# A sparse-attention and expert kernel: start-up work redistributed, fewer weight transfers, and a new planner order

## The chip, the cores and the metric

The kernel runs on one core of a Trainium2 chip. Such a core has TensorE (PE, matmuls; its weight loads stand apart as PEld), VectorE (DVE), ScalarE (ACT), GpSimd (POOL) and SyncE (SP, which here only issues DMAs and loads registers), and sixteen DMA engines. The metric is the device time of one execution in microseconds; lower is better.

## The reference, cut to what matters

Two attention layers follow each other, for B = 4 batches of S = 768 tokens in float32. The first has H = 8 heads of D = 64; tokens form 24 blocks of 32, and a block of queries sees its neighbours, the first and the last block, and three sampled blocks. The first and the last block of queries see everything.

```python
mask = np.abs(blk_i - blk_j) <= 1
mask |= (blk_i == 0) | (blk_j == 0) | (blk_i == 23) | (blk_j == 23)
for qb in range(24):
    for kb in sampled_blocks[qb]:          # 3 each
        mask[qb*32:(qb+1)*32, kb*32:(kb+1)*32] = True
x = softmax(where(mask, q @ k.T / 8, -1e9)) @ v      # heads side by side: (B, 768, 512)
# second layer: 4 experts, the best 2 per token by x @ w_gate
for e in range(4):
    a = softmax(causal((x @ wq[e]) @ (x @ wk[e]).T / 8))
    out += weight_of(e) * (a @ (x @ wv[e]) @ wo[e])
```

## The kernel before

**Steps and planner.** The kernel does not run its steps in the order of its source. Each step is handed to `Plan.add` with its engine (or a choice of engines), an estimated duration, what it reads and writes, and a priority, mostly the place of its unit in a list of units. `Plan.run` then walks through a modelled time: whenever an engine is free it takes the ready step with the lowest priority number, and the instructions are issued on each engine in just that order. On the chip every engine runs its own list strictly in order; semaphores hold an instruction back until its inputs are there. Limits in the plan: `window` (how many units ahead of the oldest unfinished one a step may be), `look` (the same for transfers), `near` (how far TensorE may reach past the first ready step for one with the same array shape, since a change of shape is costed at `SWITCH`). `AHEAD` lets score matmuls run with a priority of four units earlier.

**Stage 1, sparse attention.** For each batch, `load_keys` puts all keys into the tile `KK` (L471), `load_values` the values into `VN` with a column of ones (copies at L427 and L431; for later batches L513) and stores them to a scratch tensor `scr` in DRAM (L523). `ends` handles the first and the last block of queries for two pairs of heads (unit G): scores L671, maximum L678, exponentials L681, transposes L689, weighted sum L699, normalising L709 to L713, transpose L718. `tiles` handles 128 queries (four blocks) and four heads (unit U; two units a tile, six tiles a batch): scores L749 (first four tiles of batch 0, straight from `KK`) or L756, maximum L763, exponentials L768, transposes L774, weighted sum L788, normalising L798 to L800, transpose L805, split into two halves L443 and L444.

**What a tile needs first.** `gather_keys` copies its sampled blocks of keys to a key buffer, by block numbers read into registers (`load_registers`, L323, from the row `si`). There are three key buffers and a tile takes two. In batch 0 each block is a step of its own that POOL (L568), DVE (L568) or ACT (L566) may take. `gather_values` fills `va` and `vb`, two of each: in batch 0 POOL copies the neighbour blocks and the first and last block out of `VN` (L599, 32 to 96 partitions at a time); the sampled blocks come by one DMA each from `scr` (L640), issued on SP with block numbers from the row `sv`, in which `table` has replaced sampled blocks that another part already covers. SP reads those registers for the first tiles in four steps ahead of their use (`HOIST`); for one half tile ACT may issue the DMAs (`BYACT`).

**Setup.** `table` (L333 to L348) is one step on DVE; `registers` fills `si`; constants are made on POOL and DVE. `weights` loads `wv` with `w_gate`, `wq` with `wk`, and `wo` in 26 transfers (L414), and splits each into two halves (L418 on ACT, L420 on DVE).

**Stage 2, experts.** `project_v` (L831), `gating`, `project_qk` (L888), `expert` (scores L910 and L917, maximum L928, exponentials L931, scaling L957, transposes L967, weighted sum L984) and `project_o` (L998) follow; the units of one batch's second stage are merged in the list with the next batch's first stage. Score tiles in PSUM: two (`s`); working tiles in PSUM: four (`w`); probabilities: four (`p`).

Of the kernel before, what the change touches and what calls it, by code (L numbers as in the profile page):

```python
# [65 lines left out]
class Op:  # L66
    __slots__ = ("eng", "dur", "fn", "prio", "deps", "outs", "n", "slots", "seq", "end", "unit", "lat", "ready", "mode", "xfer", "done", "nd")


class Plan:  # L70
# [3 lines left out]
    def __init__(self, window, look, near, lat):  # L74
        self.ops, self.writers, self.window, self.look, self.near, self.lat = [], {}, window, look, near, lat
        self.now = (0, 0)
# [31 lines left out]
    def run(self):  # L108
# [3 lines left out]
        dma_free, lanes, nl = 0.0, [0.0] * 8, 0  # L112
# [11 lines left out]

        for o in self.ops:
            o.ready = 0.0
            if o.n == 0:
                push(o)
        while ndone < total:
            while fin and fin[0][0] <= t + 1e-9:  # L130
                _, _, kind, o = heapq.heappop(fin)
                if kind:
                    push(o)
                    continue
                for s in o.slots:
                    s.left -= 1
                    if s.left == 0:
                        s.drop()
                if o.unit is not None:
                    left[o.unit] -= 1  # L140
                    while head < len(order) and left[order[head]] == 0:
                        head += 1
            for e in engines:
# [76 lines left out]
def block_sparse_then_moe(ctx: ExitStack, tc: tile.TileContext, qT, kT, v, samp, wg, wq, wk, wv, wo, out):  # L220
    nc = tc.nc
# [17 lines left out]
    HOIST = [(3, 9), (9, 12), (12, 18), (18, 24)]  # L239

# [8 lines left out]
    AHEAD = 4  # L249
    pl = Plan(window=14, look=16, near=3, lat={"PE": 0.22, "ACT": 0.17, "DVE": 0.16, "POOL": 0.15, "SP": 0.1})  # L250
# [6 lines left out]
    NKG, NQ, NA = 3, 4, 4  # L257
# [32 lines left out]
    low = const.tile([128, E, E], F32, name="low")  # L290
    si = const.tile([1, NS], I32, name="si")
# [36 lines left out]
    def table():  # L328

        sf, qb, d, t = (fx(i) for i in range(4))  # L330
        v3 = lambda x: x.rearrange("p (a b) -> p a b", b=NR)
        nc.gpsimd.iota(qb, pattern=[[1, NB], [0, NR]], base=0, channel_multiplier=0, **any_dt)
        nc.vector.tensor_copy(sf, s32()[:, 0:2 * NS:2])  # L333
        nc.vector.tensor_tensor(d, sf, qb, op=ALU.subtract)
        nc.vector.tensor_tensor(d, d, d, op=ALU.mult)
        nc.vector.tensor_scalar(d, d, 1.5, None, op0=ALU.is_lt)
        nc.vector.tensor_scalar(t, sf, -0.5 * (NB - 1), None, op0=ALU.add)
        nc.vector.tensor_tensor(t, t, t, op=ALU.mult)
        nc.vector.tensor_scalar(t, t, (0.5 * (NB - 1) - 0.5) ** 2, None, op0=ALU.is_gt)
        nc.vector.tensor_tensor(d, d, t, op=ALU.max)  # L340
        for j in range(1, NR):
            for i in range(j):
                a, b_ = v3(sf)[:, :, i], v3(sf)[:, :, j]
                nc.vector.tensor_tensor(v3(t)[:, :, j], a, b_, op=ALU.is_equal)
                nc.vector.tensor_tensor(v3(d)[:, :, j], v3(d)[:, :, j], v3(t)[:, :, j], op=ALU.max)
        nc.vector.tensor_scalar(d, d, float(NB), None, op0=ALU.mult)
        nc.vector.tensor_tensor(sf, sf, d, op=ALU.max)
        nc.vector.tensor_copy(sv, sf[0:1])  # L348
# [33 lines left out]
    def rows(w, k):  # L382
        return w[k * 128:(k + 1) * 128]

    def pieces_qk(k):
        cols = lambda t, i: t[:, 0:2 * E * D].rearrange("p (a i c d) -> p a i c d", a=EP, i=2, c=2)[:, :, i]
        return [(lambda t, i=i, a=a: cols(t, i)[:, a], w[2 * a:2 * a + 2, k * 128:(k + 1) * 128].rearrange("c p d -> p c d"))
                for i, w in enumerate((wq, wk)) for a in range(EP)]

    def pieces_v(k):  # L390
        return [(lambda t: t[:, 0:E * D].rearrange("p (e d) -> p e d", e=E), wv[:, k * 128:(k + 1) * 128].rearrange("e p d -> p e d")),
                (lambda t: t[:, E * D:WVN], rows(wg, k))]
# [11 lines left out]
    def weights(at):  # L404
        for name, hi, lo, width, pieces, n in (("wv", wv_h, wv_l, WVN, pieces_v, KT),
                                               ("wqk", wqk_h, wqk_l, 2 * E * D, pieces_qk, KT),
                                               ("wo", wo_h, wo_l, DM, pieces_o, EP)):
            for k in range(n):
                s = rW.get()
                ps = pieces(k)  # L410

                def load(e, s=s, ps=ps):
                    for to, x in ps:
                        e.dma_start(to(s.t), x)  # L414

                dma(0, 0.5 * len(ps), load, both=False, r=[("vg", 0, 1)], w=[s], prio=(at, 0), xfer=1.0, nd=len(ps))
                pl.add("ACT", 0.6, lambda s=s, hi=hi, k=k, width=width:
                       nc.scalar.activation(hi[:, k], s.t[:, 0:width], AF.Copy), r=[s], w=[(name, "h", k)], prio=(at, 0))  # L418
                pl.add("DVE", 0.8, lambda s=s, hi=hi, lo=lo, k=k, width=width:
                       nc.vector.tensor_tensor(lo[:, k], s.t[:, 0:width], f(hi)[:, k], op=ALU.subtract),  # L420
                       r=[s, (name, "h", k)], w=[name], prio=(at, 0))
# [52 lines left out]
    def load_queries(b, t):  # L474
# [3 lines left out]
            r=[sts[b]["scr"]] if t and b == 0 else [], w=[(q, "raw")], xfer=1.1)  # L478
# [60 lines left out]
    def gather_keys(b, t, k):  # L539
# [30 lines left out]
        for part in [[g] for g in gs] if b == 0 else (gs[:2], gs[2:]):  # L570
# [6 lines left out]
            e, d, fn = zip(*by[:3 if b == 0 else 1])  # L577
            pl.add(e, d, fn, r=["si"] + [(k, P4) for P4 in range(HP)], w=kgs)
# [7 lines left out]
    BYACT = ((0, 0, 1),)  # L586

    def gather_values(b, t):
# [7 lines left out]
        def copies():  # L596
# [45 lines left out]
        if b == 0:  # L642
# [14 lines left out]
    def ends(b, pp_, st, X, unit):  # L657
# [16 lines left out]
        for i, (c0, cw) in enumerate(chunks):  # L674
            pl.add("PE", 0.92 if cw == 512 else 0.48, lambda i=i, c0=c0, cw=cw: sc(i, c0, cw),
                   r=[qz] + [(k, P4) for P4 in pairs], w=[ss[i]] + [(x, "r") for x in pps], unit=unit,
                   prio=(unit - AHEAD, 0), mode=(64, 64))
# [50 lines left out]
    def tiles(b, t, pp_, st, X, unit):  # L728
# [147 lines left out]
    def project_qk(X, st, p, c0, unit):  # L876
# [18 lines left out]
    def expert(b, st, p, r, unit):  # L895
# [26 lines left out]
        for i, (c0, cw) in enumerate(chunks):  # L922
# [3 lines left out]
                   unit=unit, prio=(unit - AHEAD, 0), mode=(64, 128) if c0 + cw < n else [  # L926
# [102 lines left out]
    seq = [("QZ", 0), ("K", 0, 0), ("K", 0, 1), ("V", 0), ("K", 0, 2), ("K", 0, 3), ("Q", 0, 0), ("KG", 0, 0), ("VG", 0, 0)] + ends_(0) + block(0, 0) + block(0, 1) + [("W",)] + block(0, 2) + block(0, 3)  # L1029
# [51 lines left out]

# [30 lines left out]
```

## Time and profile before

| | |
|---|---|
| runs, us | 541.57, 547.1, 542.24 (median 542.24) |
| profiled execution, us | 540.51 |
| its span, first to last instruction, us | 538.7 |
| mean granted clock of TensorE | 0.984 |
| busy share PE / PEld / DVE / ACT / POOL | 92 / 70 / 70 / 61 / 34% |
| matmuls | 8136 |
| DMA packets, volume | 58404, 70.11 MB |

The profile is one execution on the chip. A line number such as L788 is that of the listing. "Busy" counts an engine's own instructions; register loads, waits and the issuing of DMAs are not counted (they carry a q behind the engine's name, as SPq). Every idle time of an engine is put down to what ended it; "issue" means that no semaphore that the profile shows ended it.

### The profile page before, as it was taken

The numbers are of one execution on the slowest core, as the hardware profiler recorded it, in microseconds if no ns is written. First come the engines' busy times: TensorE is split into PE (matmuls) and PEld (weight loads), VectorE is DVE, ScalarE is ACT, GpSimd is POOL, SyncE is SP. The second block draws the span as 40 slices with busy tenths as digits, with TensorE's granted clock in tenths as the row PEclk, the third lists the DMA queues.
The fourth block names the chain that finished last, engine by engine and source line by source line (L and its number), as shares of the span: only waits on it lengthen the run. The fifth ranks groups of instructions, "written<-read, shape, count | busy, mean of one in ns | idle before, by whom it ended". The sixth has DMA issues, their size and how long they took to land.

```text
span 538.7 us, 20910 instructions
## 1 busy us (share of the span) xinstructions
PE 496.5 (92%) x8136; PEld 377.9 (70%) x8136; DVE 376.9 (70%) x991; ACT 329.3 (61%) x926; POOL 182.6 (34%) x449
## 2 busy tenths in 40 slices
PE   2678799897899999999999999999999999999997
PEld 1467578675667768878666778778767678778765
DVE  4677865375898875468978885457978875439783
ACT  1537774365867674566776775456776775446753
POOL 2587843243321242342241152252252132002121
PEclk9789999998999999999999999999999999999999
DMA  7553545887740178977610178878620154100011
GB/s 266 168 140 84 122 109 146 258 234 170 178 123 20 62 180 243 296 180 183 148 51 21 40 196 229 290 180 188 153 64 21 41 140 128 31 2 2 21 41 60
DMA packets 58404, 70.11 MB, mean 130 GB/s; under 512 B 17793, under 2 KB 30209, under 8 KB 58305
## 3 DMA queue, kind: packets, MB, share of 16 engines
q1 hardware_dynamic: 53296, 65.68, 45.3%
q10 hardware_dynamic: 5008, 3.09, 2.0%
q8 instruction: 65, 1.06, 0.9%
q14 instruction: 35, 0.28, 0.2%
HBM read 55.92 MB, written 12.81 MB: 128 GB/s over the span
## 4 chain that ended last, share of the span: by engine, by line
PE 75%; DVE 11%; DMA 5%; issue 3%; ACT 3%; SPq 2%; POOL 0%; ACTq 0%; POOLq 0%; DVEq 0%
PE w L888 11%; PE w L788 8%; PE w L774 8%; PE s L917 8%; PE w L984 7%; PE s L756 6%; PE w L967 6%; PE w L831 5%; PE w L998 5%; PE w L805 2%; PE w L689 2%; PE s L671 2%; PE s L749 2%; DMA pt<-in_v_dram 2%; DMA KK<-in_kT_dram 2%
## 5 line engine op out<-in xcount | busy, mean ns | idle before, releaser
L427 ACT ACTIVATE pt<-w 128x512 f32<-128x512 f32 (+3 forms) x145 | 75.0, 537 | 29.3 <-PE w L774 19.1
L957 POOL TENSOR_SCALAR p<-p,sm 128x512 f32<-128x512 f32 (+3 forms) x70 | 43.2, 625 | 145.0 <-DVE sm L944 40.2
L768 ACT ACTIVATE p<-s,sm 128x256 f32<-128x256 f32 x192 | 77.1, 483 | 20.4 <-DVE sm L763 18.9
L931 ACT ACTIVATE p<-s,sm 128x512 f32<-128x512 f32 (+3 forms) x128 | 68.4, 539 | 34.2 <-DVE sm L928 33.9
L568 POOL COPY KK<-KK 128x128 f32 x219 | 55.9, 302 | 79.8 <-PE s L756 58.3
L431 DVE COPY pt<-w 128x512 f32<-128x512 f32 (+3 forms) x95 | 56.2, 601 | 31.6 <-PE w L774 26.1
L763 DVE TENSOR_REDUCE sm<-s 128x4 f32<-128x1024 f32 x48 | 57.9, 1216 | 18.4 <-PE s L756 17.9
L928 DVE TENSOR_REDUCE sm<-s 128x2 f32<-128x512 f32 (+3 forms) x64 | 54.6, 854 | 10.0 <-PE s L917 8.8
L774 PE MATMUL w<-ident,p 128*128 128x128 f32 x384 | 56.2, 287 | 2.7 <-ACT p L768 2.2
L788 PE MATMUL w<-vb,pt 128*32 128x65 f32 x1536 | 48.8, 220 | 4.4 <-issue 4.1
L788 PE MATMUL w<-va,pt 128*32 128x65 f32 x1536 | 49.1, 223 | 3.6 <-issue 3.6
L967 PE MATMUL w<-ident,p 128*128 128x128 f32 x336 | 49.0, 279 | 3.3 <-DVE xl L444 2.0
L774 PEld LDWEIGHTS w<-ident,p 128*128 128x128 f32 x384 | 44.1, 145 | 10.9 <-ACT p L768 5.2
L917 PE MATMUL s<-qk 64*128 64x512 f32 (+3 forms) x256 | 50.3, 485 | 0.0
L554 ACT ACTIVATE KK<-KK 128x384 f32<-128x384 f32 (+3 forms) x89 | 36.4, 448 | 20.7 <-PE s L756 17.0
L967 PEld LDWEIGHTS w<-ident,p 128*128 128x128 f32 x336 | 37.4, 140 | 15.6 <-issue 4.4
L756 PE MATMUL s<-KK,q 64*32 64x256 f32 x1280 | 46.0, 385 | 1.4 <-issue 0.9
L788 PEld LDWEIGHTS w<-va,pt 128*32 128x32 f32 x1536 | 35.4, 110 | 16.1 <-issue 12.5
L984 PE MATMUL w<-pt,vb 128*64 128x128 f32 x672 | 46.4, 279 | 0.0
L888 PE MATMUL w<-xh,wqkh 128*128 128x512 f32 (+1 forms) x128 | 45.3, 354 | 0.0
L599 POOL COPY va<-VN 32x520 f32<-32x520 f32 (+2 forms) x57 | 37.2, 653 | 18.3 <-ACT VN L427 9.9
L888 PE MATMUL w<-xh,wqkl 128*128 128x512 f32 (+1 forms) x128 | 43.4, 339 | 0.0
(128 smaller groups left out, 1000.1 us busy)
## 6 DMA issues: line engine op xcount, KB each, us to landing
vb<-scr SPq DMA_DIRECT2D x267, 65.0 KB, 3.0
va<-scr SPq DMA_DIRECT2D x12, 780.0 KB, 6.8
scr<-VN SPq DMA_DIRECT2D x12, 520.0 KB, 4.6
KK<-in_kT_dram SPq DMA_DIRECT2D x16, 384.0 KB, 6.5
out_dram<-ws SPq DMA_DIRECT2D x24, 256.0 KB, 2.1
ws<-in_v_dram SPq DMA_DIRECT2D x18, 256.0 KB, 3.8
q<-in_qT_dram SPq DMA_DIRECT2D x18, 256.0 KB, 3.4
va<-scr SPq DMA_DIRECT2D x6, 585.0 KB, 6.9
```

The costliest lines, as they stand in the source:

```text
L427: nc.scalar.activation(dst(), src(), AF.Copy, scale=1.0 if mul is None else mul)
L431: nc.vector.tensor_copy(dst(), src())
L756: nc.tensor.matmul(s.t[32 * g:32 * g + 32, j, 256 * i:256 * i + 256], q.t[r, pairs[i], 32 * g:32 * g + 32], kg.t[r, i, cl(t, g)].rearrange ...
L763: pl.add("DVE", 1.16, lambda: nc.vector.tensor_reduce(sm.t[:, 0:4], s.t.rearrange("p j (t c) -> p (j t) c", t=2), AX.X, op=ALU.max, negate ...
L768: pl.add("ACT", 0.37, lambda i=i, j=j, n=n: nc.scalar.activation(pp.t[:, 256 * n:256 * n + 256], s.t[:, j, 256 * i:256 * i + 256], AF.Exp, ...
L774: nc.tensor.transpose(w.t[:, 128 * c:128 * c + 128], pp.t[:, 512 * (c // 2) + 256 * i + 128 * (c % 2):][:, 0:128], ident)
L788: nc.tensor.matmul(o.t[32 * g:32 * g + 32, VW * n:VW * n + VW], pt.t[:, 4 * i + 2 * j + c, 32 * g:32 * g + 32], x.t[:, cl(t, g), h * VW:h ...
L888: nc.tensor.matmul(w.t[:, 0:cw], a[:, k, x], y[:, k, c0:c0 + cw], start=n == 0, stop=n == 3 * KT - 1)
L917: nc.tensor.matmul(ss[i].t[:, j, 0:cw], qk.t[x, 0, r * 128:(r + 1) * 128], qk.t[x, 1, c0:c0 + cw], start=not mask_first, stop=mask_first o ...
L931: pl.add("ACT", 0.26 + 0.00083 * cw, lambda i=i, j=j, c0=c0, cw=cw: nc.scalar.activation(pps[j].t[:, p0[j] + c0:p0[j] + c0 + cw], ss[i].t[ ...
L967: nc.tensor.transpose(w.t[:, 128 * i:128 * i + 128], pps[j].t[:, p0[j] + 128 * t:][:, 0:128], ident)
L984: nc.tensor.matmul(o.t[64 * j:64 * j + 64, 0:128], vb.t[:, t, e * D:(e + 1) * D], pts[j].t[:, t0s[j] + t], start=t == 0, stop=t == r, tile ...
```

## The change

1. **Sampled keys of the first two tiles by POOL alone.** For tiles 0 and 1 of batch 0 the steps of `gather_keys` may only go to POOL; the registers for their seven blocks are read by POOL in seven steps of their own ahead (`HOIST_K`).
2. **Function table asked for at once.** A one-element exponential on ACT, on a tile that DVE zeroes, stands among the first steps.
3. **Block table in parts.** `table` becomes four steps on DVE with priority 9.5 instead of one with -2; its iota is a step on POOL; SP's register reads get priority 3.5 instead of -1.
4. **Weights in 15 transfers.** `w_gate` comes in one, `wv` in four, `wq` and `wk` in eight (all four experts at once, columns laid out accordingly in `project_qk`), `wo` in two.
5. **First and last block of the values for tile 1** come by two DMAs from `VN` instead of eight POOL copies; ACT's share of sampled values is dropped (`BYACT` empty); the second tile's queries are loaded after the keys instead of after the stored values.
6. **Order drawn anew.** `window` 24 instead of 14, `look` 20 instead of 16; scores ahead by 7 (tiles), 4 (experts), 5 (ends) instead of 4; the plan's DMAs begin at 3.5 us; and TensorE leaves a step of another array shape waiting when one of the present shape becomes ready within 0.09 us.

```diff
-    def __init__(self, window, look, near, lat):
+    def __init__(self, window, look, near, lat, keep):
-        dma_free, lanes, nl = 0.0, [0.0] * 8, 0
+        dma_free, lanes, nl = 3.5, [0.0] * 8, 0
+        def better(e, o, i):
+            if not self.keep.get(e):
+                return False
...
+            if e == "PE":
+                if mode is None or any(m[0] == mode for m in o.mode):
+                    return False
+                return any(x.ready - t < self.keep[e] and any(m[0] == mode for m in x.mode) and x.prio[0] <= o.prio[0] + self.near
+                           for x in soon[e])
...
+                        if pick is None and better(e, o, x[3]):
+                            skipped.append(x)
+                            continue
...
+    HOIST_K = [(c, c + 3) for c in range(3, 24, 3)]
-    AHEAD = 4
-    pl = Plan(window=14, look=16, near=3, lat={...})
+    TUNE = dict(window=24, look=20, near=3, u=7, e=4, g=5, keep={"PE": 0.09}, byact=0, dm=(1,), wat=2)
...
+    pl.add("DVE", 0.1, lambda: nc.vector.memset(warm, 0.0), w=["warm"], prio=(-4, 0))
+    pl.add("ACT", 1.4, lambda: nc.scalar.activation(warm, warm, AF.Exp), r=["warm"], w=["table"], prio=(4, 0))
-    pl.add("DVE", 3.0, table, r=[(t0, "s32")], w=["sv"], prio=(-2, 1))
+    pl.add("POOL", 0.5, blocks_numbered, w=[(t0, 0)], prio=(-2, 0))
+    for i, n in enumerate((1.0, 0.9, 1.3, 0.8)):
+        pl.add("DVE", n, lambda i=i: table(i), r=[(t0, "s32"), (t0, i)], w=[(t0, i + 1)] + ["sv"] * (i == 3), prio=(9.5, i))
     for c in HOIST:
-        pl.add("SP", 1.5, lambda c=c: load_registers(SP, sv, *c), r=["sv"], w=[("held", c)], prio=(-1, 0))
+        pl.add("SP", 1.5, lambda c=c: load_registers(SP, sv, *c), r=["sv"], w=[("held", c)], prio=(3.5, 0))
+    for c in HOIST_K:
+        pl.add("POOL", 0.8, lambda c=c: load_registers(POOL, si, *c), r=["si"], w=[("keys", c)], prio=(-1, 0))
...
+        return [(lambda t, i=i: t[:, E * D * i:E * D * (i + 1)].rearrange("p (e d) -> p e d", e=E),
+                 w[:, k * 128:(k + 1) * 128].rearrange("e p d -> p e d")) for i, w in enumerate((wq, wk))]
...
+        dma(0, 0.5, lambda e: e.dma_start(gv(), wg.rearrange("(k p) e -> p k e", p=128)), both=False, r=[("vg", 0, 1)], w=[g],
+            prio=(at, 0), xfer=0.2)
...
-            r=[sts[b]["scr"]] if t and b == 0 else [], w=[(q, "raw")], xfer=1.1)
+            r=[] if b or t == 0 else [(sts[b]["k"], HP - 1)] if t == 1 else [sts[b]["scr"]], w=[(q, "raw")], xfer=1.1)
-            e, d, fn = zip(*by[:3 if b == 0 else 1])
+            e, d, fn = zip(*by[:3 if b == 0 and t > 1 else 1])
-    BYACT = ((0, 0, 1),)
+    BYACT = ((0, 0, 1),) if TUNE["byact"] else ()
+            def ends_of(x, i, dst, key):
+                y = VN[0][32 * (i % 4):32 * (i % 4) + 32, i // 4].rearrange("p h c -> p (h c)")
+                dma(b, 0.6, lambda e: e.dma_start(dst.t[96:128, x[0]:x[-1] + 1], sub_ap(y, 0, [y.ap[0], [0, len(x)], [1, R]])),
+                    r=[vn] if t == 0 else [vn, ("vg", 0, t - 1)], w=[key], xfer=0.25 * len(x))
+            if t in TUNE["dm"]:
+                ends_of(in_va, 0, va, (va, 0))
+                ends_of(in_vb, NB - 1, vb, (vb, "s"))
-            pl.add("PE", ..., prio=(unit - AHEAD, 0), mode=(64, 32))
+            pl.add("PE", ..., prio=(unit - TUNE["u"], 0), mode=(64, 32))
```

More of the change, by code (lines that the diff above doesn't have):

```diff
@@ L66 @@
 class Op:
-    __slots__ = ("eng", "dur", "fn", "prio", "deps", "outs", "n", "slots", "seq", "end", "unit", "lat", "ready", "mode", "xfer", "done", "nd")
+    __slots__ = ("eng", "dur", "fn", "prio", "deps", "outs", "n", "slots", "seq", "end", "unit", "lat", "ready", "mode", "xfer", "done", "nd", "ns")
 class Plan:
-    def __init__(self, window, look, near, lat):
+    def __init__(self, window, look, near, lat, keep):
         self.ops, self.writers, self.window, self.look, self.near, self.lat = [], {}, window, look, near, lat
+        self.keep = keep
         self.now = (0, 0)
@@ L123, in push @@
                 heapq.heappush(wait[e], (o.prio, o.seq, o, i))
+        soon = {e: [] for e in engines}
         for o in self.ops:
-            o.ready = 0.0
+            o.ready, o.ns = 0.0, o.n
             if o.n == 0:
                 push(o)
+        def better(e, o, i):
+            if not self.keep.get(e):
+                return False
+            d = o.dur[i]
+            d = 1.0 if callable(d) else d
+            if e == "PE":
[3 more added lines that the diff above has]
+                           for x in soon[e])
+            return any(x.prio < o.prio and len(x.eng) == 1 and x.ready - t < self.keep[e] * (t + d - x.ready) for x in soon[e])
         while ndone < total:
@@ L132, in run @@
                 if kind:
+                    for e in o.eng:
+                        soon[e].remove(o)
                     push(o)
@@ L247, in f @@
         return ap.bitcast(F32)
-    AHEAD = 4
-    pl = Plan(window=14, look=16, near=3, lat={"PE": 0.22, "ACT": 0.17, "DVE": 0.16, "POOL": 0.15, "SP": 0.1})
+    TUNE = dict(window=24, look=20, near=3, u=7, e=4, g=5, keep={"PE": 0.09}, byact=0, dm=(1,), wat=2)
+    pl = Plan(window=TUNE["window"], look=TUNE["look"], near=TUNE["near"], lat={"PE": 0.22, "ACT": 0.17, "DVE": 0.16, "POOL": 0.15, "SP": 0.1}, keep=TUNE["keep"])
     def ring(name, n, shape, dt=F32, space=None, ordered=False):
@@ L290, in block_sparse_then_moe @@
     low = const.tile([128, E, E], F32, name="low")
+    warm = const.tile([128, 1], F32, name="warm")
     si = const.tile([1, NS], I32, name="si")
@@ L326, in fresh_registers, with blocks_numbered, table @@
         return vals
-    def table():
+    def blocks_numbered():
+        nc.gpsimd.iota(fx(1), pattern=[[1, NB], [0, NR]], base=0, channel_multiplier=0, **any_dt)
+    def table(part):
         sf, qb, d, t = (fx(i) for i in range(4))
         v3 = lambda x: x.rearrange("p (a b) -> p a b", b=NR)
[L332 to L348, printed above, removed]
@@ new lines, in table @@
+        if part == 0:
+            nc.vector.tensor_copy(sf, s32()[:, 0:2 * NS:2])
+            nc.vector.tensor_tensor(d, sf, qb, op=ALU.subtract)
+            nc.vector.tensor_tensor(d, d, d, op=ALU.mult)
+            nc.vector.tensor_scalar(d, d, 1.5, None, op0=ALU.is_lt)
+        elif part == 1:
+            nc.vector.tensor_scalar(t, sf, -0.5 * (NB - 1), None, op0=ALU.add)
+            nc.vector.tensor_tensor(t, t, t, op=ALU.mult)
+            nc.vector.tensor_scalar(t, t, (0.5 * (NB - 1) - 0.5) ** 2, None, op0=ALU.is_gt)
+            nc.vector.tensor_tensor(d, d, t, op=ALU.max)
+        elif part == 2:
+            for j in range(1, NR):
+                for i in range(j):
+                    a, b_ = v3(sf)[:, :, i], v3(sf)[:, :, j]
+                    nc.vector.tensor_tensor(v3(t)[:, :, j], a, b_, op=ALU.is_equal)
+                    nc.vector.tensor_tensor(v3(d)[:, :, j], v3(d)[:, :, j], v3(t)[:, :, j], op=ALU.max)
+        else:
+            nc.vector.tensor_scalar(d, d, float(NB), None, op0=ALU.mult)
+            nc.vector.tensor_tensor(sf, sf, d, op=ALU.max)
+            nc.vector.tensor_copy(sv, sf[0:1])
@@ L576, in gather_keys @@
                   ("ACT", 0.8 + 0.7 * m, lambda part=part: sampled(nc.scalar, ACT, part))]
-            e, d, fn = zip(*by[:3 if b == 0 else 1])
-            pl.add(e, d, fn, r=["si"] + [(k, P4) for P4 in range(HP)], w=kgs)
+            e, d, fn = zip(*by[:3 if b == 0 and t > 1 else 1])
+            pl.add(e, d, fn, r=["si"] + [(k, P4) for P4 in range(HP)] + [("keys", (c, c + m * NR))] * ((c, c + m * NR) in HOIST_K and b == 0),
+                   w=kgs)
         for h, kg in enumerate(kgs):
@@ L676, in ends @@
                    r=[qz] + [(k, P4) for P4 in pairs], w=[ss[i]] + [(x, "r") for x in pps], unit=unit,
-                   prio=(unit - AHEAD, 0), mode=(64, 64))
+                   prio=(unit - TUNE["g"], 0), mode=(64, 64))
             pl.add("DVE", 0.09 + 0.00208 * cw, lambda i=i, cw=cw: nc.vector.tensor_reduce(
```

44 lines of the change are left out of this document (25 added, 19 removed).

## The prediction

> **What bounds the kernel now.** The page comes first: its span, and TensorE's busy share in forty slices of 13.5 us.
>
> ```profile
> span 538.7 us, 20910 instructions
> ...
> PE   2678799897899999999999999999999999999997
> ```
>
> From the twelfth slice on TensorE is busy nine tenths or more; the gaps stand in the first eleven. The view that cuts the span into stages gives them in microseconds (stretch and length; busy time of PE, weight loads, VectorE, ScalarE, GpSimd; clock, DMA share, GB/s).
>
> ```profile
> 8.00:38.00 30.00, 19.39 (x302) 13.70 (x306) 21.31 (x56) 14.58 (x37) 17.12 (x31) 0.84 0.57 183
> 38.00:70.00 32.00, 26.14 (x849) 20.96 (x846) 25.95 (x59) 22.02 (x63) 24.50 (x46) 0.94 0.47 114
> 70.00:100.00 30.00, 29.19 (x498) 23.41 (x497) 16.09 (x33) 14.92 (x37) 10.74 (x19) 1.00 0.58 155
> 100.00:140.00 40.00, 33.87 (x678) 25.38 (x675) 25.43 (x59) 24.16 (x63) 15.77 (x51) 0.96 0.86 221
> 140.00:520.00 380.00, 372.79 (x5733) 284.06 (x5723) 277.19 (x747) 245.44 (x704) 108.51 (x283) 1.00 0.45 118
> ```
>
> TensorE idles 10.6 us of 8 to 38, 5.9 of 38 to 70, 6.1 of 100 to 140, and only 7.2 of the 380 us after that. So the body is bound by TensorE's own order, the start by what feeds it. The timeline shows where (start, length, in brackets the idle time before and what ended it).
>
> ```profile
> 7.90 3.34 PE L671 MATMUL s<-KK,qz 64*64 64x512 f32 x16 [7.90 <-DVE qz L433]
> ...
> 14.75 3.00 PE L689 MATMUL w<-ident,p 128*128 128x128 f32 x12 [3.51 <-ACT p L681]
> ...
> 26.23 3.04 PE L749 MATMUL s<-KK,q 64*32 64x192 f32 x128
> ...
> 37.83 0.44 PE L788 MATMUL w<-va,pt 128*32 128x65 f32 x8
> ```
>
> L749 is the first tile's scores, L788 its first weighted sum: at 37.83 the steady work begins. The gaps also cost clock, as the 0.57 behind the wait of 3.51 shows (the third number from the end):
>
> ```profile
> 14.00:18.00 4.00, 3.25 (x20) 2.39 (x22) 2.44 (x5) 3.58 (x10) 3.13 (x8) 0.57 0.29 103
> ```
>
> At the mean clock of 0.84 in 8 to 38, 19.4 busy us hold 16% or 3.1 us that full clock would save. The stretch thus has 10.6 + 3.1 = 13.7 us to give, and 16.3 us of full-clock work.
>
> **The change part by part.** The other engines at the start:
>
> ```profile
> 1.79 1.25 ACTq L518 DMA_DIRECT2D pt<-in_v_dram  x2
> ...
> 5.90 1.57 SPq L471 DMA_DIRECT2D KK<-in_kT_dram  x2
> ...
> 7.87 0.18 DVE L333 CAST p<-p 128x72 f32<-128x72 int32 x1
> ...
> 11.58 1.28 ACT L427 ACT_TABLE_LOAD   x1 [11.58 <-DMA pt<-in_v_dram]
> 11.64 1.80 DVE L678 TENSOR_REDUCE sm<-s 128x2 f32<-128x1024 f32 x2
> 12.88 1.15 ACT L427 ACTIVATE VN<-pt 128x512 f32<-128x512 f32 x2
> ...
> 13.57 1.40 POOL L599 COPY va<-VN 96x520 f32<-96x520 f32 x2 [9.93 <-ACT VN L427]
> ...
> 20.01 1.23 DVE L568 COPY KK<-KK 128x128 f32 x3 [2.09 <-DMA scr<-VN]
> ...
> 20.82 0.71 ACT L566 ACTIVATE KK<-KK 128x128 f32 x3 [2.59 <-DVE KK L568]
> ...
> 22.21 3.98 SPq L640 DMA_DIRECT2D vb<-scr  x8
> ...
> 28.18 0.83 POOL L568 COPY KK<-KK 128x128 f32 x3 [5.46 <-issue]
> ...
> 29.07 6.58 POOL L599 COPY va<-VN 32x520 f32<-32x520 f32 x10
> ...
> 29.42 2.49 ACTq L640 DMA_DIRECT2D vb<-scr  x3
> ...
> 54.66 6.12 POOL L599 COPY va<-VN 32x520 f32<-32x520 f32 x9 [2.39 <-PE w L788]
> ```
>
> *Block table in parts.* VectorE computes the table without a break from 7.87, and the first maximum (L678) comes right behind it at 11.64. In four pieces of about 0.9 us with a late priority, the table lets the maximum start when its scores are there, the first eight of L671's sixteen, near 9.8: up to 1.8 us. Nothing is lost, since VectorE waits for the next scores anyway. SyncE's register loads, which need the table, must then only be done before L640.
>
> *Function table at once.* The load's 1.28 us stand between the landing of the values and ScalarE's first copy; asked for at the start, they lie beside the first transfers, behind which ScalarE has nothing to compute until 11.1. Values and exponentials come 1.3 earlier. The Trainium skill (ScalarE: Activation LUTs, What ACT_TABLE_LOAD costs) puts about 1.38 us of draining on top of 1283 ns, which would make it an estimated 2.7. Here the copy at 12.88 follows the load directly, so the row is used.
>
> *Keys by GpSimd alone.* Each engine that copies sampled keys must first load block numbers into registers (min/median/max ns):
>
> ```profile
> L323 POOLq TENSOR_LOAD <-si x6: 728/740/2117, 14.3 to 59.3; - x6
> L323 DVEq TENSOR_LOAD <-si x6: 746/756/2712, 17.0 to 55.5; - x6
> ```
>
> The load of 2.7 us at 17.0 keeps VectorE idle for 2.09 us, and ScalarE has 2.59 idle us before its keys, just where the first two units need both. Those go, and for the first two tiles the later loads too. GpSimd gets seven loads of 0.74 = 5.2 us, covered by its 9.93 idle us before 13.57; were they late, tile 0's keys would be late by as much. It copies seven blocks at 0.8, where it did two: 4.0 us more. Of its 17 value copies for the second tile eight at 0.66 = 5.3 us become two DMAs. Net 1.3 us less.
>
> *Order at the start.* GpSimd's 5.46 idle us before 28.18 are a wait for L749: a tile holds two of three key buffers, so tile 1's keys wait for tile 0's scores. With scores up to seven units ahead (four before), L749 can run when keys and queries are there. *ScalarE's three value DMAs* (29.42) go to SyncE, 3 × 0.52 = 1.6 us there, and ScalarE is rid of 2.5 us ahead of the first exponentials. The second queries are loaded after the keys, not after the stored values; if that issue stands on ScalarE's queue before the keys land, copies and exponentials wait behind it, and I take off 0.5 us.
>
> The new first weighted sum follows from three feeders; the landings of keys, values and stored values in us (min/median/max):
>
> ```profile
> DMA to landing us min/median/max: 5.9/6.9/7.3
> ...
> DMA to landing us min/median/max: 9.2/9.3/11.9
> ...
> DMA to landing us min/median/max: 2.9/3.9/4.7
> ```
>
> 1. GpSimd: the last keys, issued near 7.2, land at 14.5; three blocks at 0.8 and eleven value copies at 0.66 give 14.5 + 2.4 + 7.3 = 24.2.
> 2. Sampled values: the last values, issued near 2.4, land at 14.3; copied by 15, the store lands 4.7 later at 19.7, where L640 starts at 22.2 now; nine DMAs at 0.52 and about 2.5 for the last to land (between the 2.9 of a store and less) give 26.9.
> 3. TensorE: 16.3 us of work from 8 with three or four waits of 0.5 to 1 end near 27.
>
> So L788 starts near 27 instead of 37.8: 10.8 us. Does it last? GpSimd then has tile 1's four key blocks (3.2), copies for tiles 1, 2 and 3 (9 + 12 + 9 at 0.66 = 19.8) and a third of the keys of 2 and 3 (2.4): 24.2 + 25.4 = 49.6, where tile 3's copies end at 54.66 + 6.12 = 60.8 now: 11.2. TensorE needs 26.1 us less 6% of slow clock for the next stage, and 27 + 24.5 plus half of its 5.9 idle us is 54.5 against 70. So it lasts. From 10.8 I take the 0.5 above and 1.5 for a slower GpSimd: **8.8 us**. The 1.5 is from these rows:
>
> ```profile
> 78.19 4.33 POOL L599 COPY va<-VN 32x520 f32<-32x520 f32 x5
> 78.46 0.88 DVE L420 TENSOR_TENSOR wqkl<-ws,wqkh 128x512 fp32r<-128x512 f32 x1
> ```
>
> Five copies took 4.33 us beside L420, where the ten at 29.07 took 6.58: 0.87 against 0.66 each. Over 20 copies and seven blocks it could cost from 0 to 20 × 0.21 + 2 = 6; VectorE's early work mostly reads PSUM instead, so 1.5. The Trainium skill has the rule, and it speaks against this change: GpSimd shares its SBUF interfaces with VectorE and contends with instructions of two SBUF inputs or in a two-port mode (GPSIMD Engine Reference, Key points). By that rule the price depends on what VectorE runs beside the copies.
>
> *Weights in 15 transfers.*
>
> ```profile
> L414 SPq DMA_DIRECT2D ws<-in_wq_dram x8: 386/437/467, 61.7 to 73.5; - x8
> ```
>
> Eleven issues fewer at about 0.45 free 5 us of SyncE around 61 to 74; the bytes stay. TensorE is busy 29 of 30 us from 70 to 100, which hides it, so it counts nothing; without that cover it is worth up to 5.
>
> *Order in the body.* What a new order can win is TensorE's changes of array shape:
>
> ```profile
> 92.32 0.38 PE L805 MATMUL w<-ident,xn 128*128 128x128 f32 x2
> 92.54 0.60 PE L774 MATMUL w<-ident,p 128*128 128x128 f32 x4
> ...
> 145.67 0.44 PE L805 MATMUL w<-ident,xn 128*128 128x128 f32 x2
> 146.04 1.62 PE L699 MATMUL w<-VN,pt 128*64 128x65 f32 x48
> ```
>
> Between equal shapes two transposes take 0.22 us from start to start, between two other shapes 0.37: 0.075 a change. With 48 tile, 48 expert and 8 end units of three or four changes each there are some 350 (26 us). Now TensorE holds for a same-shape step due within 0.09 us; that may save one in twenty, 1.3 us. The bounds: 70 saved (+5), 50 added (-4), since the farther look-ahead reshuffles everything.
>
> The sum: 8.8 + 1.3 = 10.1 us. The profiled execution took 540.51 us, the span and 1.8 around it; it becomes 530.4. The median of the runs shown is 1.7 above it at 542.24, so the forecast is **532 us**.
>
> **The rivals.** *GpSimd becomes the bound.* With the full 6 us of contention the start gains 10.8 - 0.5 - 6 = 4.3 and the body 1.3, so 5.6: near 537. For it: blocks leave engines that had room. Against: eight copies leave GpSimd. The Trainium skill's GPSIMD page is the rule behind this case. *The gain is given back at the seam of the batches.* There TensorE already stands still in the middle of a unit:
>
> ```profile
> 129.53 0.22 PE L788 MATMUL w<-va,pt 128*32 128x65 f32 x1 [3.58 <-issue]
> ```
>
> The DMA share is 0.86 from 100 to 140. If the larger look-ahead bunches the second batch's transfers there, the 6.1 idle us become 14 and the time is 540. Against it: those loads wait for buffers that the first batch frees, so they should shift with it. *Slower:* scores run seven units ahead keep the two score buffers and the four for probabilities, and other units find none. If each of 48 tile units waited 0.4 us, 19 us would be lost: 551; the sign turns by more than 1% from 0.32 each. For it: there are only two score buffers. Against: with scores four ahead TensorE is busy 98%. *More in the body:* 70 changes saved and the start at 11 to 13: 525. *The table load is not early*, because the warm-up queues behind ScalarE's DMA issues: 1.3 us, inside the range.
>
> **How the numbers follow.** Forecast (528 to 536) 0.55; GpSimd 0.17; seam 0.13; slower 0.06; more in the body 0.09. The range of 524 to 540 (gains of 18 and of 2) leaves out the slow case, half of the seam and a little of the last. One per cent, 5.4 us, is about what a measurement of this kernel tells from no change. Faster by more (below 536.8): 0.55 + 0.09 and half of GpSimd's, 0.73. Within 1%: the rest of GpSimd's and the seam, 0.21. Slower: 0.06.
>
> **What the changed profile would show.** Right: the table load before 5 us; L678 near 10; no L566 before 26; the first L749 near 18, the first L788 near 27; full clock in 24 to 38; over 26 busy us of 32 in 38 to 70; fewer rows of L414. Wrong: L788 late behind GpSimd's copies, a wait of TensorE over 5 us between 90 and 130, or over 10 idle us in the 380 of the body.

## The result and the profile after

The changed kernel takes **527.64 us** (median; 525.93 to 534.0) against 542.25 in the runs of before beside it: a ratio of 0.970, 95% interval 0.962 to 0.978. A repeat of the same kernel gave 527.36 (525.35 to 529.18), ratio 0.973, interval 0.969 to 0.977. Medians are of all runs and ratios of the undisturbed ones, and as the profile that came with the result is of a disturbed execution (534.0), all lines of "after" are the repeat's, whose profiled execution took 529.18, with a span of 527.3.

In the changed kernel's listing L678 became L733, L681 L736, L689 L744, L713 L768, L718 L773, L749 L804, L768 L823, L774 L829, L788 L843, L566 L608, L568 L610, L599 L642, L640 L695, L523 L565, L323 L348. Its stages, in the columns of the prediction's first view by stage:

```profile
8.00:38.00 30.00, 24.23 (x498) 17.55 (x497) 23.47 (x57) 18.64 (x47) 17.59 (x41) 0.97 0.70 215
38.00:70.00 32.00, 28.20 (x777) 21.41 (x764) 27.80 (x66) 24.47 (x66) 22.15 (x42) 0.93 0.48 113
70.00:100.00 30.00, 28.14 (x542) 22.37 (x542) 14.04 (x34) 14.36 (x32) 11.47 (x19) 1.00 0.77 223
100.00:140.00 40.00, 36.07 (x706) 27.35 (x694) 28.94 (x79) 27.20 (x73) 15.36 (x54) 1.00 0.79 202
140.00:520.00 380.00, 372.92 (x5619) 285.55 (x5618) 268.17 (x741) 246.65 (x717) 107.61 (x276) 1.00 0.43 115
```

Length less the first busy number is TensorE's idle time; busy times one minus clock is what the clock costs.

| stage, us | idle before → after | clock loss before → after | won |
|---|---|---|---|
| 8 to 38 | 10.61 → 5.77 | 3.10 → 0.73 | 7.2 |
| 38 to 70 | 5.86 → 3.80 | 1.57 → 1.97 | 1.7 |
| 70 to 100 | 0.81 → 1.86 | 0 → 0 | -1.0 |
| 100 to 140 | 6.13 → 3.93 | 1.35 → 0 | 3.5 |
| 140 to 520 | 7.21 → 7.08 | 0 → 0 | 0.1 |

The sum is 11.5, the difference of the spans 11.4 (538.7 - 527.3). That they agree so well is luck: the clock is shown to two digits, and a 1.00 over 380 us can hide almost 2 us. In the changed kernel it hides this stretch:

```profile
310.00:320.00 10.00, 9.29 (x128) 7.30 (x127) 4.37 (x11) 5.36 (x16) 4.09 (x12) 0.83 0.62 195
```

That is 9.29 × 0.17 = 1.6 us of clock. So the long body gives nothing or loses 1.5, the start gives 8.9 and the seam of the first two batches 3.5, and some 1.5 us of the 11.4 has no place in the table. Who kept TensorE waiting at the start, from the view of waits from 8 to 70 (us in total, times, longest); before:

```profile
PE w L718 <- DVE ws L713: 5.4, 2, 2.8
PE w L689 <- ACT p L681: 5.0, 2, 3.5
PE w L788 <- issue: 3.3, 4, 1.2
PE w L774 <- ACT p L768: 1.4, 2, 1.2
```

After:

```profile
PE w L829 <- ACT p L823: 3.8, 2, 2.5
PE w L744 <- ACT p L736: 2.6, 1, 2.6
PE w L843 <- issue: 1.0, 2, 0.7
...
PE w L773 <- DVE ws L768: 0.3, 1, 0.3
```

The waits for the normalising of the ends (L718 behind L713) fell from 5.4 to 0.3, and that for their exponentials by half. But one wait has grown, that for a tile's exponentials (1.4 in L774 before, 3.8 in L829). The timeline of the changed kernel shows what stands there:

```profile
3.04 1.28 ACT L405 ACT_TABLE_LOAD   x1 [3.04 <-issue]
...
11.57 1.20 DVE L733 TENSOR_REDUCE sm<-s 128x2 f32<-128x1024 f32 x1
...
13.85 2.79 PE L744 MATMUL w<-ident,p 128*128 128x128 f32 x12 [2.61 <-ACT p L736]
...
21.27 2.31 PE L804 MATMUL s<-KK,q 64*32 64x192 f32 x124
...
22.81 0.62 POOL L642 COPY vb<-VN 32x520 f32<-32x520 f32 x1
...
29.69 2.39 PE L804 MATMUL s<-KK,q 64*32 64x192 f32 x128
...
32.00 0.83 DVE L610 COPY KK<-KK 128x128 f32 x3 [1.29 <-DMA vb<-scr]
32.02 0.87 ACT L608 ACTIVATE KK<-KK 128x128 f32 x3 [1.94 <-DMA vb<-scr]
32.75 1.21 DVE L818 TENSOR_REDUCE sm<-s 128x4 f32<-128x1024 f32 x1
...
34.62 1.62 PE L829 MATMUL w<-ident,p 128*128 128x128 f32 x8 [2.54 <-ACT p L823]
36.17 2.03 PE L804 MATMUL s<-KK,q 64*32 64x192 f32 x64
38.13 0.44 PE L843 MATMUL w<-va,pt 128*32 128x65 f32 x8
```

The first weighted sum still starts at 38.13 (37.83 before). What changed is how much TensorE has done by then: the scores of two tiles and part of a third stand ahead of it. The key copies for the third tile still go to ScalarE and VectorE, each behind a register load of its own; ScalarE's:

```profile
L348 ACTq TENSOR_LOAD <-si x1: 906/906/906, 30.8 to 30.8; - x1
```

The key buffer comes free in the middle of the second tile's scores (near 29.69 + 1.2 = 30.9; r8 below shows that release), but ScalarE's load ends at 31.7 and its first copy (L608) follows at 32.02; the row names a DMA as releaser. VectorE's load (30.1, 0.99 us long) ended at 31.1, and what held its copy (L610) until 32.00, the DMA that the row names or another, was not tried. The maximum of the second tile's first scores (L818) stands behind that copy and ends at 33.96, the exponentials follow at 34.11, and TensorE waits 2.54 us.

### The profile page after: what moved, and what is told of

It is laid out like the page before. It is cut to its first block, busy times and chain, and to the rows that moved or that the text cites. A ratio compares the mean times of both kernels' runs of the same rounds, so it can differ in the third digit from the quotient of the medians.

```text
span 532.2 us, 20854 instructions
## 1 busy us (share of the span) xinstructions
PE 494.0 (93%) x8136; PEld 378.4 (71%) x8136; DVE 364.2 (68%) x980; ACT 333.8 (63%) x936; POOL 177.4 (33%) x446
## 4 chain that ended last, share of the span: by engine, by line
PE 69%; DVE 12%; DMA 5%; ACT 4%; issue 3%; POOL 3%; SPq 2%; POOLq 0%; ACTq 0%; DVEq 0%
PE w L943 10%; PE s L972 7%; PE w L843 7%; PE w L1039 7%; PE w L829 7%; PE w L1022 6%; PE s L811 6%; PE w L1053 6%; PE w L886 6%; DVE sm L983 2%; DMA vb<-scr 2%; POOL va L642 2%; PE s L726 2%; PE w L860 2%; DMA KK<-in_kT_dram 2%
## 5 line engine op out<-in xcount | busy, mean ns | idle before, releaser
L1012 POOL TENSOR_SCALAR p<-p,sm 128x512 f32<-128x512 f32 (+3 forms) x73 | 44.6, 621 | 165.6 <-DVE sm L999 46.5
L469 ACT ACTIVATE pt<-w 128x512 f32<-128x512 f32 (+3 forms) x157 | 81.5, 549 | 22.4 <-PE w L829 9.9
L823 ACT ACTIVATE p<-s,sm 128x256 f32<-128x256 f32 x192 | 78.0, 487 | 16.1 <-DVE sm L818 13.0
L610 POOL COPY KK<-KK 128x128 f32 x231 | 58.2, 298 | 50.2 <-PE s L811 32.3
L473 DVE COPY pt<-w 128x512 f32<-128x512 f32 (+3 forms) x83 | 47.0, 577 | 25.7 <-PE w L829 17.5
L983 DVE TENSOR_REDUCE sm<-s 128x2 f32<-128x1024 f32 (+3 forms) x64 | 54.2, 853 | 11.2 <-PE s L972 10.6
L818 DVE TENSOR_REDUCE sm<-s 128x4 f32<-128x1024 f32 x48 | 57.7, 1214 | 5.6 <-PE s L811 4.4
L829 PE MATMUL w<-ident,p 128*128 128x128 f32 x384 | 54.6, 281 | 7.3 <-ACT p L823 3.8
L829 PEld LDWEIGHTS w<-ident,p 128*128 128x128 f32 x384 | 43.6, 143 | 14.6 <-ACT p L823 5.0
L843 PE MATMUL w<-vb,pt 128*32 128x65 f32 x1536 | 49.5, 220 | 2.9 <-DMA vb<-scr 1.8
L843 PE MATMUL w<-va,pt 128*32 128x65 f32 x1536 | 49.8, 223 | 2.3 <-issue 2.3
L1022 PE MATMUL w<-ident,p 128*128 128x128 f32 x336 | 49.1, 280 | 2.6 <-DVE p L1011 0.9
L1039 PEld LDWEIGHTS w<-pt,vb 128*64 128x64 f32 x672 | 36.1, 137 | 16.5 <-issue 6.7
L843 PEld LDWEIGHTS w<-va,pt 128*32 128x32 f32 x1536 | 36.6, 109 | 15.4 <-issue 8.6
L811 PE MATMUL s<-KK,q 64*32 64x256 f32 x1280 | 44.4, 382 | 0.3 <-ACT p L823 0.3
L596 ACT ACTIVATE KK<-KK 128x256 f32<-128x256 f32 (+3 forms) x84 | 34.5, 458 | 15.4 <-DMA KK<-in_kT_dram 10.5
L943 PE MATMUL w<-xl,wqkh 128*128 128x512 f32 (+1 forms) x128 | 43.5, 340 | 0.0
```

What stands on the lines that cost most here:

```text
L469: nc.scalar.activation(dst(), src(), AF.Copy, scale=1.0 if mul is None else mul)
L610: e.tensor_copy(dst, src)
L811: nc.tensor.matmul(s.t[32 * g:32 * g + 32, j, 256 * i:256 * i + 256], q.t[r, pairs[i], 32 * g:32 * g + 32], kg.t[r, i, cl(t, g)].rearrange ...
L823: pl.add("ACT", 0.37, lambda i=i, j=j, n=n: nc.scalar.activation(pp.t[:, 256 * n:256 * n + 256], s.t[:, j, 256 * i:256 * i + 256], AF.Exp, ...
L829: nc.tensor.transpose(w.t[:, 128 * c:128 * c + 128], pp.t[:, 512 * (c // 2) + 256 * i + 128 * (c % 2):][:, 0:128], ident)
L843: nc.tensor.matmul(o.t[32 * g:32 * g + 32, VW * n:VW * n + VW], pt.t[:, 4 * i + 2 * j + c, 32 * g:32 * g + 32], x.t[:, cl(t, g), h * VW:h ...
```

## Experiments

Theories at the outset: **A**, the new parts free the start, as the prediction has it; **B**, the planner's new settings make the body's order better; **C**, any new order moves the time by several us, and this one is a lucky draw. The last two columns are TensorE's idle time in each kernel's profiled execution, from the view by stage. Beside r5 to r8 the kernel before took 540.47, beside r9 to r12 540.56; ratios are to the runs alongside. The intervals are 3 to 9 us wide, so differences between medians of some 3 us or less rest on the profiles.

| run | parts | settings | us, median (lowest to highest) | ratio, 95% | idle 8 to 70 | idle 140 to 520 |
|---|---|---|---|---|---|---|
| before (beside r1 to r4) | old | old | 541.64 (538.62 to 546.83) | | 16.5 | 7.2 |
| r6 | old | old, redrawn | 552.97 (551.14 to 553.61) | 1.016 to 1.029 | 16.5 | 16.0 |
| r2 | new | old | 546.36 (545.28 to 547.0) | 1.006 to 1.013 | 11.1 | 15.5 |
| r7 | new | old, redrawn | 542.4 (539.42 to 546.85) | 0.999 to 1.008 | 11.4 | 15.1 |
| r3 | old | new | 535.55 (530.88 to 538.77) | 0.980 to 0.992 | 13.6 | 7.8 |
| r1 | new | new | 527.36 (525.35 to 529.18) | 0.969 to 0.977 | 9.6 | 7.1 |
| r5 | new | new, redrawn | 527.19 (523.45 to 530.29) | 0.968 to 0.984 | 10.1 | 4.6 |
| r10 | new | new, old window | 528.47 (526.37 to 532.25) | 0.973 to 0.985 | 11.7 | 5.3 |
| r11 | new | new, old ahead | 534.99 (530.04 to 538.98) | 0.982 to 0.990 | 11.9 | 12.1 |
| r12 | new | new, no holding | 534.9 (531.22 to 539.44) | 0.988 to 0.994 | 10.6 | 10.5 |
| r4 | keys on three engines | new | 530.13 (528.2 to 532.95) | 0.973 to 0.983 | 13.3 | 6.8 |
| r8 | third tile's keys on GpSimd | new | 530.38 (527.32 to 535.31) | 0.971 to 0.987 | 12.1 | 7.5 |
| r9 | table load late | new | 529.71 (527.02 to 532.19) | 0.975 to 0.984 | 12.1 | 6.5 |

**The parts with the old settings (r2), and the settings with the old parts (r3).**

```diff
 # r2: changed kernel
-    TUNE = dict(window=24, look=20, near=3, u=7, e=4, g=5, keep={"PE": 0.09}, ...)
+    TUNE = dict(window=14, look=16, near=3, u=4, e=4, g=4, keep={}, ...)
-        dma_free, lanes, nl = 3.5, [0.0] * 8, 0
+        dma_free, lanes, nl = 0.0, [0.0] * 8, 0
 # r3: kernel before, with the holding rule and the new settings put in
```

Expected of r2: 

> All the changed parts, but the planner with its settings of before (window 14, look 16, scores ahead by 4, no holding, transfers from 0). Theory A: the parts make the start faster by themselves, 529 to 533 us. Theory B: without the new order little is left, 538 to 542. Theory C: anywhere between.

Expected of r3: 

> The kernel before with the planner's new settings alone (window 24, look 20, scores ahead by 7, 4 and 5, holding within 0.09 us, transfers from 3.5). Theory A: 538 to 543 us, no difference from before. Theory B: 528 to 533, most of the gain. Theory C: anywhere, slower than before included.

r3 lies between what A and B expected: 6.1 us are won, and they are not in the body (7.8 idle us, 7.2 before). r2, at 546.36, is slower than any of the three theories had it. Its stages contradict A as a whole, but not its step on the start:

```profile
8.00:38.00 30.00, 22.98 (x467) 16.50 (x472) 23.88 (x59) 17.77 (x45) 18.14 (x42) 0.97 0.68 211
38.00:70.00 32.00, 27.96 (x862) 22.23 (x846) 27.58 (x66) 21.12 (x61) 24.45 (x47) 0.92 0.48 117
...
140.00:520.00 380.00, 364.53 (x5550) 276.12 (x5548) 261.44 (x704) 232.93 (x676) 106.08 (x273) 1.00 0.43 114
```

At the start 5.4 idle us of 16.5 are gone, and behind 140 us 8.3 are added. Was that loss the old settings', or this draw's?

**The same kernels drawn anew (r5, r6, r7).** One harmless number, the delay that the planner assumes behind a ScalarE instruction, changes the order of the body and hardly that of the start:

```diff
-    lat={"PE": 0.22, "ACT": 0.17, ...}
+    lat={"PE": 0.22, "ACT": 0.19, ...}
```

Expected of r5: 

> The changed kernel, its whole order drawn anew by a harmless number: the planner assumes 0.19 us instead of 0.17 after a ScalarE instruction. The start keeps its order (TensorE's first 580 steps are the same). If the order of the body is a matter of luck (theory C), the start's idle time of TensorE from 8 to 70 us stays at 9 to 11 us, while the idle time from 140 us to the end moves by several us and the time lies anywhere between 525 and 536. If the new settings make good orders by themselves (theory B), the idle time after 140 us stays within 1 us of the 10.7 of the changed kernel, and the time within 2 us of 527.4.

Expected of r6: 

> The kernel before with the same harmless number changed (0.19 us instead of 0.17 assumed after a ScalarE instruction), parts and settings old. The order is the same for TensorE's first 117 steps and another one behind. Theory C: the kernel before was one draw among many; idle time after 140 us moves from its 10.9 by several us, and the time lies anywhere between 535 and 550. Theory B: old settings give one level, within 2 us of 541.6. If it comes out near 535 by the draw alone, then the 6 us that the new settings won with the old parts are no proof for the settings.

Expected of r7: 

> All new parts with the old settings, as in the run that came out at 546.4, drawn anew by the same harmless number. In that run TensorE stood idle 11.1 us from 8 to 70 (16.5 before) but 19.6 from 140 us to the end (10.9 before). Theory C: the loss behind 140 us was this draw's; a new draw brings it down by 4 us or more, and the time to 536 to 542, with the start's gain of about 5 us of idle time kept. Theory B: the old settings with the new parts always lose there, and the time stays within 2 us of 546.

The kernel before, redrawn, loses 12.5 us, more than either theory had; its body:

```profile
140.00:520.00 380.00, 363.98 (x5608) 274.10 (x5607) 260.72 (x702) 234.68 (x669) 104.07 (x276) 1.00 0.43 118
```

TensorE is idle 16.0 us there, as in r2 (15.5) and r7 (15.1, in the slowest of its ten executions, 546.85), not 7.2. So of four orders with the old settings three stand idle for 15 to 16 us in the body, and the kernel before is the exception. Those 8.8 us are not all of r6's loss; and r7's median fell 4.0 below r2's with the body's idle time as it was, which no theory expected. The changed kernel, redrawn, keeps its time, and its body is at 4.6, lower by more than the 1 us that B allowed:

```profile
140.00:520.00 380.00, 375.40 (x5659) 288.25 (x5657) 270.50 (x752) 249.86 (x722) 106.19 (x273) 1.00 0.43 117
```

C is right about the old settings (two draws 12.5 us apart with the old parts, 4.0 with the new ones) and, as far as one redrawing tells, wrong about the new ones (0.2 apart). B fits best, though not for the prediction's reason: the settings did not improve on the body of before, but the three orders drawn with all of them (r1, r3, r5) have one as good. Three orders against four make that likely, not certain. Compared draw for draw, the parts win 8.2 us with the new settings (535.55 to 527.36), 4.0 of it as idle time from 8 to 70; with the old ones the two draws with new parts lie 6.6 and 10.6 below the redrawn kernel before and at or above the lucky one.

**Which setting (r10, r11, r12).**

```diff
 # r10
-    TUNE = dict(window=24, look=20, ...)
+    TUNE = dict(window=14, look=16, ...)
 # r11
-    TUNE = dict(..., u=7, e=4, g=5, ...)
+    TUNE = dict(..., u=4, e=4, g=4, ...)
 # r12
-    TUNE = dict(..., keep={"PE": 0.09}, ...)
+    TUNE = dict(..., keep={}, ...)
```

Expected of r10: 

> The changed kernel with one pair of the planner's settings as before: 14 units between the oldest open unit and the newest (24 in the changed one), 16 for transfers (20). Idle time of TensorE from 140 to 520 us was 4.6 to 7.8 in three kernels with the new settings and 15 to 16 in three of four with the old ones. If the window is what spares the body, that idle time goes to 15 and the time to 535 or more; if not, it stays under 8 and the time under 530.

Expected of r11: 

> The changed kernel with scores asked for four units ahead as before (seven for tiles and five for whole-row units in the changed one). If this is what spares the body, the idle time from 140 to 520 goes to 15 and the time to 535 or more. By the prediction's step on the start, scores four ahead also hold back the first tile's scores: then the idle time from 8 to 70 rises from 9.6 to about 11, as in the runs with all old settings, and the time by 1.5 us at least. The prediction's slower rival (scores seven ahead hold the two score buffers) would have it faster than 527.

Expected of r12: 

> The changed kernel without the rule that lets TensorE hold up to 0.09 us for a step of the same array shape. The prediction gave this rule 1.3 us by fewer changes of shape. The changed kernel has 321 changes, the kernel before 320, so I now expect no fewer changes for it (315 to 330 without it) and a time within 2 us of 527.4; if this rule is what spares the body, the idle time from 140 to 520 goes to 15 and the time to 535 or more.

The window is worth nothing that shows (1.1 us). Scores ahead and holding show 7.6 and 7.5, more than r12 was expected to. In r11 more idle time stands in the body and at the start:

```profile
140.00:520.00 380.00, 367.86 (x5569) 280.28 (x5568) 266.47 (x728) 236.18 (x688) 109.94 (x281) 1.00 0.43 115
```

That is 12.1 idle us against 7.1, and 11.9 against 9.6 from 8 to 70. For r12 the profiled execution was the fastest of ten (531.22), and its idle time behind 140 us is 3.4 above r1's; the rest of the 7.5 no profile here shows. TensorE changes its array shape 318 times in r12 and 321 in r1, so holding does not work by fewer changes. How it works, and whether the two sizes would stand in another draw, is open: each is one order. The transfers planned from 3.5 us were not put back by themselves.

**Keys on three engines (r4).** Every order is the changed kernel's; the seven key blocks of the first two tiles are issued on GpSimd, VectorE and ScalarE, without the register loads ahead.

```diff
 # tiles 0 and 1: third block DVE, fourth ACT, tile 1's first ACT, others POOL
-("POOL", cost, lambda part=part: sampled(nc.gpsimd, POOL, part))
+("POOL", cost, lambda part=part: sampled(*engine_of(t, part), part))
```

Expected: 

> The changed kernel with every other instruction in the same order on each engine, but the seven key blocks of tiles 0 and 1 on GpSimd, VectorE and ScalarE as before, each with its own register loads just ahead. Theory A: the stalls on VectorE and ScalarE come back, 3 to 6 us slower than the changed kernel. Theory B: within 1.5 us of it.

The time rises by 2.8 us and the idle time at the start by 3.7. The waits from 8 to 70 have grown, each a little, where the key copies stand ahead of what TensorE needs:

```profile
PE w L744 <- ACT p L736: 3.2, 2, 2.7
PE w L843 <- issue: 2.7, 3, 1.2
PE s L804 <- issue: 1.1, 1, 1.1
```

**The third tile's keys on GpSimd too (r8).** The grown wait at 34.62 suggests it.

```diff
-("DVE", ..., sampled(nc.vector, DVE, part)), ("ACT", ..., sampled(nc.scalar, ACT, part))
+("DVE", ..., sampled(nc.gpsimd, POOL, part)), ("ACT", ..., sampled(nc.gpsimd, POOL, part))   # t == 2
```

Expected: 

> The changed kernel, every order as it was, but the four sampled key blocks of the third tile (its first two had them on VectorE and ScalarE) are emitted on GpSimd. In the changed kernel ScalarE and VectorE stand 1.9 and 1.3 us before these copies until 32.0 us (key buffers held by the second tile's scores), the exponentials behind them come late, and TensorE waits 2.5 us at 32.1 to 34.6. If theory A is right that key copies on the other engines stall the start, that wait falls to 1.2 us or less, and the time falls by 1 to 2 us, to 525.5 to 526.5. If GpSimd becomes the bound, its four blocks with register loads (4 x (0.74 + 0.86) = 6.4 us against 5.6 idle us there) push its value copies back and the time stays or rises by up to 2 us.

In the timeline the first of these copies starts when scores release it; in the view of waits from 8 to 70 the wait for exponentials shrinks from 3.8 to 2.2, and another takes its place:

```profile
30.71 0.76 POOL L610 COPY KK<-KK 128x128 f32 x3 [2.76 <-PE s L804]
```

```profile
PE s L804 <- POOL KK L610: 2.4, 2, 1.3
PE w L829 <- ACT p L823: 2.2, 2, 1.3
```

The scores now wait for GpSimd's key copies, and the time is 3.0 higher, where 2 was the most expected. The intervals of r4 and r8 overlap that of r1 a little; the new waits carry the verdict. In this order two tiles on GpSimd is the better place between. Both runs keep an order drawn up for the changed kernel; what an order drawn for their own split of the copies would take was not tried.

**The table load late (r9).** Every order is the changed kernel's, without the small exponential at the start.

```diff
-    pl.add("ACT", 1.4, lambda: nc.scalar.activation(warm, warm, AF.Exp), ...)
+    pl.add("ACT", 1.4, lambda: None, ...)
```

Expected: 

> The changed kernel, every order as it was, without the tiny exponential that asks for the function table at the start. The 1.28 us load then stands again behind the landing of the values, just ahead of ScalarE's first copy at 11.5 us. If step 2 is right that this costs what the load lasts, the first exponentials and transposes come 1.3 us later and the time rises by up to 1.3 us, to about 528.7; the Trainium skill's draining would make it an estimated 2.7, 530. If the first maxima, which end only after VectorE's table (12.8 us), set the exponentials anyway, the time stays within 0.5 us of 527.4.

ScalarE's and TensorE's rows of the timeline:

```profile
11.55 1.28 ACT L469 ACT_TABLE_LOAD   x1 [11.55 <-DMA pt<-in_v_dram]
12.84 1.67 ACT L469 ACTIVATE VN<-pt 128x512 f32<-128x512 f32 x3
...
15.23 2.79 PE L744 MATMUL w<-ident,p 128*128 128x128 f32 x12 [3.88 <-ACT p L736]
...
26.30 0.30 PE L804 MATMUL s<-KK,q 64*32 64x64 f32 x4 [1.35 <-issue]
```

The wait ahead of L744 is 3.88 instead of 2.61, the load's 1.28; the last four score matmuls wait 1.35 instead of 0.33, and the profile shows no releaser. Together 2.3, and the time is 2.35 higher, twice what was expected; the intervals of r9 and r1 overlap a little here too, and the waits carry the verdict.

**A repeat of the changed kernel (r1)**, its code as it is. Expected: 

> The changed kernel once more, for a profile that no disturbance lengthens. Theory A (the start): the lead over the kernel before is 9 us or more by the end of the first batch's sparse tiles and stays; about 527 us. Theory B (the order of the body): the lead is 4 to 6 us there and grows by 8 or more in the steps after 140 us. Theory C (luck of the draw): the lead comes and goes by several us from stage to stage.

It gave 527.36, and the profile used above.

## Why the prediction was right, and where it was not

Forecast 532, measured 527.6: inside the range, faster as forecast. Its sum was 10.1 where the profiles differ by 11.3 (540.51 and 529.18) and the medians by 14.6; r1's profiled execution is the slowest of its six, so no profile shows the rest. The mechanism of the start, less waiting on its feeders, held. That the sum came so near is in part luck: its 1.3 for the body was nothing, the seam's 3.5 was not in it, and two of the steps under the 8.8 failed, as follows.

*The start, 8.8.* Right in size: 8.9 from 8 to 70. Wrong in the mark it was hung on: the first weighted sum was to start near 27 and starts at 38.13. It was read as the point where steady work begins; the new order fills TensorE with other tiles' scores and transposes ahead of it (24.23 busy us at 0.97 instead of 19.39 at 0.84). What was won is work done, not the place of one instruction.

*Sampled values, 26.9.* The step failed at the store. It was costed as issued by 15 and landed 4.7 later. The three stores are issued 1.4 earlier, and take longer; before and after:

```profile
L523 SPq DMA_DIRECT2D scr<-VN x3: 395/403/618, 16.2 to 17.4; - x3
...
DMA to landing us min/median/max: 2.9/3.9/4.7
```

```profile
L565 SPq DMA_DIRECT2D scr<-VN x3: 392/395/809, 14.8 to 15.8; - x3
...
DMA to landing us min/median/max: 2.9/4.3/6.1
```

So the sampled values begin at 15.8 + 6.1 = 21.9, as before (22.21): the earlier issue was given back in the transfer. The issue itself hangs on SyncE's register loads: of the four that stood ahead of the stores before (the last from 14.8 to 16.0), one now stands behind them, and a store that landed sooner would have met it:

```profile
L348 SPq TENSOR_LOAD <-sv x1: 3974/3974/3974, 16.7 to 16.7; - x1
```

It ends at 20.6, so at most 1.3 us were there to be won by a quicker store.

*Block table in parts, up to 1.8.* Nothing: L733 starts at 11.57. VectorE runs the four parts in one go, in the old order, so the lower priority moved nothing.

*Function table, 1.3.* The mis-sized term: 2.35 in r9, in two waits of 1.27 and 1.02 more. The load's length was right at the first wait; the delay then met a second one. The Trainium skill (ScalarE: Activation LUTs, What ACT_TABLE_LOAD costs) gave an estimated 2.7, nearer in sum, but its draining is not what the trace shows: the copy follows the load at 12.84, 0.01 behind its end.

*Keys by GpSimd.* Right: without it 2.8 us (r4), the size of the 2.09 and 2.59 us stalls that it rested on. Tile 0's value copies ended at 23.4 (22.81 + 0.62), forecast 24.2. The later loads were not all gone: the third tile's copies bring the stall back at 30.8 to 32 us.

*Contention, 1.5.* Not there. In the groups of 13 to 62 us the copies cost the same; before and after:

```profile
L599 POOL COPY va<-VN 32x520 f32<-32x520 f32 x34 | 21.6, 637 | 4.0 <-PE w L788 2.4
```

```profile
L642 POOL COPY va<-VN 32x520 f32<-32x520 f32 x35 | 22.1, 630 | 1.8 <-PE w L843 0.2
```

The rule of the Trainium skill (GPSIMD Engine Reference, Key points) names the kind of VectorE instruction that contends; what ran on VectorE beside the early copies here did not slow them on the mean.

*Weights, 0.* Not tried by itself. TensorE's idle time from 70 to 100 went from 0.81 to 1.86; nothing is seen of a gain. Nor were tile 1's two value DMAs, ACT's dropped DMAs and the earlier queries tried alone.

*Body, 1.3.* Wrong twice. Shape changes are 321 against 320, so the term is 0; what the holding wins in r12's comparison comes another way. And the step took the body of before as given, when it was a draw that three of four old-setting orders do not reach: on the orders tried the settings are not worth 1.3 us on top, they keep some 8 idle us from being lost. The bounds (+5, -4) were too narrow for that.

*Seam.* The rival had it the wrong way round: 3.5 were won there, and 1.0 was lost just ahead of it. What won it is open; r6, with old parts and settings, is idle for only 3.0 us from 100 to 140 (6.1 before), so a draw alone can do it. *Slower,* by score buffers held: r11 says the opposite in its one order, four ahead is 7.6 us worse. *GpSimd the bound* did not happen, but r8 shows how near it is: four blocks more and its copies end the scores' wait.

Of the marks given: table load before 5 (3.04), no key copy on ScalarE before 26 (32.02) and over 26 busy us in 38 to 70 (28.20) were right; L733 near 10, L804 near 18 (21.27), L843 near 27 and full clock in 24 to 38 were not; that last stretch had 0.93:

```profile
24.00:38.00 14.00, 11.17 (x278) 8.87 (x277) 10.11 (x22) 10.75 (x30) 7.94 (x20) 0.93 0.62 157
```

## What to carry to other kernels

Where a program draws up the order, a change of any part is also a new draw: redraw both kernels with a harmless number before a difference is put down to the part, because one such number moved the kernel before by 12.5 us here. Sum what a start costs as idle time and lost clock over the stage, not as the time of one instruction that marks it, since the order around that mark can change. A step made earlier on its queue is only won if the transfer behind it is quicker too: check where it lands.

## What the runs showed of the hardware

A store of the same size took up to 6.1 us to land when issued at 14.8 to 15.8 us, and up to 4.7 at 16.2 to 17.4; the DMA share from 8 to 38 us was 0.70 and 0.57. Whether the fuller engines are the cause was not tried. One register load on SyncE, right behind these stores, took 3.97 us where the three ahead of them took 0.68 to 1.46; why was not tried either. And a delay of 1.28 us on one engine's queue showed as 2.3 us of waits on another (r9).
